# Scatters of routed rows issued one by one, each behind a read of Y, instead of in bursts of four

## The chip, the cores and the metric

The kernel runs on one core of a Trainium2 chip. The metric is device time in microseconds: the median of three timed runs of the kernel before is 1020.86 us (1019.78 to 1023.98). TensorE multiplies matrices (its weight loads are shown apart, as PEld), VectorE (DVE) and ScalarE (ACT) work on tiles, GpSimd (POOL) does small fills and copies and issues indirect transfers, and SyncE (SP) issues the plain ones.

## The reference

Three stages in a row, in float32, on 4 x 768 = 3072 tokens:

- a recurrent attention: per head a 40 x 40 state is read by `r` (that gives the output `y`), then decayed by `w`, corrected by `a` and `b`, and gets `v k^T` added, token by token;
- a mixture of experts: each row of 320 goes through the one of 8 experts (320 to 1024 to 320, ReLU) that has the largest of 8 logits, and is scaled by its probability and an output gate;
- a shared block, 320 to 2048 to 320, with a learned slope for negative values.

```
y[:, :, t] = einsum('bhd,bhde->bhe', rt, state)
logits = x @ w_gate;  e_idx = argmax(logits, axis=1)
out[mask] = gate_w[mask, None] * eom[mask, e, None] * (maximum(x[mask] @ w1[e], 0) @ w2[e])
```

## The kernel before

**Attention.** The recurrence is cut into 12 chunks of 64 tokens; each chunk is done in two halves of 8 (batch, head) pairs a side. That makes 24 steps, and `slot(s)` (line 717) is called for s = 0 to 24: it does the state part of step s and the read part (Y) of step s - 1, which I call the Y part of step s. For the first sixteen steps it also prepares step s + 8 (cumulative decays, triangular factors, and the inversion of 32x32 blocks, `tmp` and `S`, lines 668 and 669, which VectorE does in small pieces between the rest). The inversion's tile S is cleared by GpSimd (lines 658 and 659) once in four steps. From step 17 on (`LATE`) there is nothing more to prepare.

In the Y part TensorE transposes (`XT`, line 757), multiplies by R (`MY`, line 766) and forms two masked products (`pp`, lines 770 and 771, VectorE writes them into the tile x); after the state part's products `R` (lines 687, 728 and 789) and `W` (line 739, from `rh`, which ScalarE evicts, line 731) it adds the rest of MY (line 809). VectorE then updates the state (`tm` and `mc`, lines 714 and 715) and reads Y out of PSUM into `yt` in two halves (line 814). The next loads of X and R (lines 692 and 702) are issued by SP at that place. Next comes the R product of the next step (line 728), which waits for `yt` and for the state.

**Routing inside the scan.** Every second chunk completes 256 rows a half; `unit` (line 116) turns them into rows of 320 and their logits: TensorE multiplies (line 123), VectorE sums the logits (line 124), ScalarE copies the rows into a buffer `xu` (line 126, a ring of four). `route` (line 128) returns the work on four such units as a list of small jobs: find the best expert, count with a triangular matrix, `place` (each row's position in its expert's list), four scatters, `sums` and `scale`. A scatter (line 174) is one indirect transfer by GpSimd of 128 rows of 320 floats to the DRAM array `xs`, followed by a memset of one element, `gap`. The jobs wait in the queue `rq`, and `slot` takes a few at its end (lines 842 to 845): a step takes `best`, the next `count`, the next `place` and then up to three scatters, the next the fourth scatter and `sums`, the next `scale`. From step 17 one more job is taken in the middle of a step (line 783). So the scatters of a group of four units are issued in one burst; there are five such groups. The last two groups, of two units each, are routed in step 24 and after it.

**After the scan.** `xload(0)` (line 198) is called after step 23 and loads the rows of expert 0 from `xs`; it waits for all scatters issued so far. GpSimd copies their last columns (line 207), TensorE transposes them (line 374), and the experts follow. Weights are loaded by SP (line 297) into three raw buffers from step 20 on and split into two parts by ScalarE, VectorE or GpSimd (lines 300 and 301).

The order of the instructions on each engine is the order in which the program issues them; waits between engines follow from the tiles that they read and write.

Of the kernel before, what the change touches and what calls it, by code (L numbers as in the profile page):

```python
# [11 lines left out]
F32 = mybir.dt.float32  # L12
# [16 lines left out]
NST = 2 * NCH  # L29
NUN = 2 * NCH  # L30
# [42 lines left out]
class Moe:  # L73
# [6 lines left out]
    def init(s,ap,rp):  # L80

        nc=s.nc; cp=s.cp; a=s.a; s.rp=rp

        s.wg=ap.tile([128,4,96],F32,name="wg")
        s.lg=rp.tile([128,8,16],F32,name="lg")
        s.pos=cp.tile([128,24],I32,name="pos"); s.sc=cp.tile([128,24],F32,name="sc")
        s.tot=cp.tile([128,NE+1],F32,name="tot"); nc.gpsimd.memset(s.tot,0.0)
        def iota(t,pattern,base=0,ch=0): nc.gpsimd.iota(t,pattern=pattern,base=base,channel_multiplier=ch,allow_small_or_imprecise_dtypes=True)
        s.nbk=-(-(NT-CB)//128)
        s.io=cp.tile([128,1],F32,name="io"); iota(s.io,[[0,1]],0,1)  # L90
        s.al=cp.tile([128,16],F32,name="al")
        s.scat=[]; s.gap=cp.tile([1,1],F32,name="gap"); s.xu={}
        s.oh=cp.tile([128,24,NE],F32,name="ohs"); s.pf=cp.tile([128,24],F32,name="pf")
        s.ids=cp.tile([128,24],I32,name="ids")
        nc.gpsimd.iota(s.ids,pattern=[[128,6],[768,4]],base=0,channel_multiplier=1)
        s.ido=rp.tile([128,24],F32,name="ido"); iota(s.ido,[[128,6],[768,4]],OVF,1)

        s.tri=rp.tile([128,128],F32,name="tri"); nc.gpsimd.memset(s.tri,1.0)
        nc.gpsimd.affine_select(out=s.tri,in_=s.tri,pattern=[[1,128]],base=-1,channel_multiplier=-1,compare_op=ALU.is_ge,fill=0.0)
        s.one=cp.tile([128,128],F32,name="one"); nc.gpsimd.memset(s.one,1.0)  # L100
        s.rev=rp.tile([128,NE],F32,name="rev"); iota(s.rev,[[-1,NE]],NE)
        s.base=rp.tile([128,NE],F32,name="base"); iota(s.base,[[CAP,NE]],CA+CB-CAP); nc.gpsimd.memset(s.base[:,0:1],0.0)
        s.end=rp.tile([128,NE],F32,name="end"); iota(s.end,[[CAP,NE]],CA+CB); nc.gpsimd.memset(s.end[:,0:1],float(CA))
# [12 lines left out]
    def unit(s,n,yt,ps,wk):  # L116
        nc=s.nc
        for u in range(2):

            t=ps.tile([128,512],F32,tag="ps",name="xtp"); tp=t[:,0:384].rearrange("t (p g) -> t p g",p=4)  # L120
            if n==22 and u==0:
                for _ in range(4): nc.tensor.matmul(t[:,384:512],s.ident,s.ident,start=True,stop=True)
            for p in range(4): nc.tensor.matmul(tp[:,p],yt[:,4*u+p],s.wg[:,p],start=True,stop=True)  # L123
            nc.vector.tensor_reduce(s.lg[:,(n+u)%8],tp.rearrange("t p g -> t g p")[:,80:96],AX.X,ADD)
            x=s.xu[n+u]=s.rp.tile([128,D],F32,name=f"xu{u}") if n+2==NUN else wk.tile([128,D],F32,tag="xu",name="xu",bufs=4)
            nc.scalar.copy(x.rearrange("t (p d) -> t p d",p=4),tp[:,:,0:80])

    def route(s,n0,n1,ps,wk):

        nc=s.nc; N=n1-n0; V=nc.vector; last=n1==NUN; sx=f"{n0}" if n0>=NUN-4 else ""  # L130
        if sx: wk=s.rp
        t={}
        def T(nm,k=NE):
            t[nm]=wk.tile([128,N,k] if k else [128,N],F32,tag="rt_"+nm+(sx if nm=="ex" else ""),name=nm,bufs=1)
            return t[nm]
        lg=s.lg[:,n0%8:n0%8+N]; l=lg[:,:,0:NE]; z=lg[:,:,NE:]
        bc=lambda x: x.unsqueeze(2).to_broadcast([128,N,NE])
        bm=lambda x: x.unsqueeze(1).to_broadcast([128,N,NE])
        f=lambda x: x.rearrange("p n e -> p (n e)")
        oh=s.oh[:,n0:n1]  # L140
        def best():
            if n0==4*(NCH//2-1):

                V.tensor_copy(s.tot[:,NE:NE+1],s.tot[:,0:1]); V.memset(s.tot[:,0:1],0.0)
                V.memset(s.base[:,0:1],float(CA)); V.memset(s.end[:,0:1],float(CA+CB))
            mx=T("mx",0); V.tensor_reduce(mx,l,AX.X,ALU.max)
            d=T("d"); V.tensor_tensor(d,l,bc(mx),SUB)
            v=T("v"); V.scalar_tensor_tensor(v,d,0.0,bm(s.rev),ALU.is_equal,MUL)
            m2=T("m2",0); V.tensor_reduce(m2,v,AX.X,ALU.max)
            V.tensor_tensor(oh,v,bc(m2),ALU.is_equal)  # L150
        def count():
            pr=s.mp.tile([128,2,N,NE],F32,tag="tp",name="pr") if last else ps.tile([128,2,N,NE],F32,tag="ps",name="pr")
            nc.tensor.matmul(f(pr[:,1]),s.one,f(oh),start=True,stop=True)
            nc.tensor.matmul(f(pr[:,0]),s.tri,f(oh),start=True,stop=True)
            c=t["pr"]=wk.tile([128,2,N,NE],F32,tag="rt_pr",name="prs",bufs=1)
            nc.scalar.copy(c,pr)
            nc.scalar.activation(T("ex"),t["d"],AF.Exp)
            v=T("v"); V.tensor_tensor(v,oh,bm(s.end),MUL)
            V.tensor_reduce(T("le",0),v,AX.X,ADD)
        def place():  # L160
            pr=t["pr"]

            run=wk.tile([128,N+1,NE],F32,tag="rt_run",name="run",bufs=1)
            V.tensor_tensor(run[:,0],s.tot[:,0:NE],s.base,ADD)
            for i in range(N):
                V.tensor_tensor(run[:,i+1],run[:,i],pr[:,1,i],ADD)
            rk=T("v"); V.tensor_tensor(rk,pr[:,0],run[:,0:N],ADD)
            V.tensor_tensor(rk,rk,oh,MUL)
            pf=s.pf[:,n0:n1]; V.tensor_reduce(pf,rk,AX.X,ADD)
            m2=T("m2",0); V.tensor_tensor(m2,pf,t["le"],ALU.is_ge)  # L170
            V.tensor_tensor(m2,m2,s.ido[:,n0:n1],MUL)
            V.tensor_tensor(s.pos[:,n0:n1],pf,m2,ALU.max)
            V.tensor_tensor(s.tot[:,0:NE],run[:,N],s.base,SUB)
        def scatter(n):
            i=nc.gpsimd.indirect_dma_start(out=s.xs,out_offset=IOA(s.pos[:,n:n+1]),in_=s.xu.pop(n),in_offset=None)

            for o in s.scat: s.tc.declare_no_dep(i.ins,o.ins,reason="distinct rows")
            s.scat.append(i)
            nc.gpsimd.memset(s.gap,0.0)
        def sums():  # L180
            zz=T("zz"); V.tensor_tensor(zz,z,oh,MUL)
            V.tensor_reduce(T("zs",0),zz,AX.X,ADD)
            sm=T("sm",0); V.tensor_reduce(sm,t["ex"],AX.X,ADD)
            V.tensor_scalar(sm,sm,1e-9,None,ADD)
        def scale():
            ez=T("ez",0); nc.scalar.activation(ez,t["zs"],AF.Exp,scale=-1.0)
            V.scalar_tensor_tensor(ez,ez,1.0,t["sm"],ADD,MUL)
            V.reciprocal(s.sc[:,n0:n1],ez)
        return [(0,best),(0,count),(0,place)]+[(1,lambda n=n: scatter(n)) for n in range(n0,n1)]+[(1,sums),(2,scale)]

    def rows(s,e):
        o,n=((0,CA),(CA,CB))[e//NE] if e%NE==0 else (CA+CB+CAP*(e-1),CAP)
# [345 lines left out]
def attention(ctx,octx,tc,a,m,ident,rp):  # L538
# [178 lines left out]
    def slot(s):  # L717
# [31 lines left out]
        if Y:  # L749
# [3 lines left out]
            for sd in range(2):  # L753
# [2 lines left out]
                for qq in range(4):  # L756
                    nc.tensor.transpose(XT[:,qq],x1[bl,sd,qq,64:192],ident[bl,bl])
                nc.scalar.copy(xt[:,:,192*sd:192*sd+64],XT)
            if not B: route(1000); units()

            MY=[ps.tile([P,2,208],F32,tag="ps",name="MY") for _ in range(2)]
            def y2(t): return bass.AP(t.tensor,t.offset,[*t.ap[:-1],(144,2),(1,64)])
# [4 lines left out]
            def pp(sd):  # L767
                Pp=ps.tile([P,8,64],F32,tag="ps",name="Pp")
                for qq in range(4):
                    nc.tensor.matmul(Pp[:,2*qq:2*qq+2],xt[:,qq,128*sd:128*sd+128],rz1[:,:,qq,sd],start=True,stop=True)  # L770
                nc.vector.tensor_tensor(p4(x1[:,sd]),Pp.rearrange("p (a j) t -> p a j t",j=2),mask.unsqueeze(1).unsqueeze(1).to_broadcast([P,4,2,64]),MUL)  # L771
            def p4(t): return bass.AP(t.tensor,t.offset,[t.ap[0],(232,4),(PO[1]-PO[0],2),(1,64)])
            ym(0,YA)
            if not B: route(1)
# [29 lines left out]
        if Y:  # L804
# [8 lines left out]
            for b in range(2):  # L813
                i=nc.vector.tensor_tensor(v4(yt[:,4*b:4*b+4,cs]),y2(MY[b]),v4(e1[:,4*b:4*b+4,0:64]),MUL)
                if n2 is None: fence[0]=i
            if not B:
                while rq and rq[0][1].__name__!='sums': route(1)
            if s+1<NST: loadX(s+1); loadR(s+1)
# [24 lines left out]
        route(1)  # L843
        for _ in range(3):
            if rq and rq[0][0]==1: route(1)
    ready=[]; rq=deque(); YA=4
    def units():
        while ready:
            c2,up,yt=ready.pop(0)
            m.unit(4*c2+2*up,yt,ps,wk)  # L850
            n=4*c2+2*up+2
            if up or c2==5:
                new=m.route(n-(4 if c2<5 else 2),n,ps,wk)

                k=len(new)-2 if n==NUN else 0
                for j in reversed(new[:k]): rq.appendleft(j)
                rq.extend(new[k:])
    def route(n):
        for _ in range(min(n,len(rq))): rq.popleft()[1]()
# [82 lines left out]
```

## Time and profile before

| what | value |
|---|---|
| median of three timed runs | 1020.86 us |
| profiled execution, its own time | 1029.33 us |
| its span, first to last instruction | 1027.6 us |
| mean granted TensorE clock | 0.946 |
| TensorE, VectorE, ScalarE, GpSimd busy | 958.8, 779.2, 398.3, 148.5 us |
| scan with routing | about the first 430 us |

The profile page gives busy time by engine and the costliest groups of instructions; the trace behind it answers questions on a stretch of time. In a timeline row the first number is the start in microseconds from the span's start, the second the time that the row covers, then the engine, the line, the operation, output and inputs by name, the shapes and the count; in brackets stand the idle time of the engine before it and what ended it. [...] A row of a step begins with the window (from the start of one step's first `yt` product to the start of the next step's) and its length; the steps shown are 8, 9, 12, 16, 17, 19, 20, 21 and 23, and counts stand in brackets behind the busy times. "issue" is time in which an engine waited for nothing that the profile shows.

### The profile page before, as it was taken

The numbers are of one execution on the slowest core, as the hardware profiler recorded it, in microseconds if no ns is written. First come the engines' busy times: TensorE is split into PE (matmuls) and PEld (weight loads), VectorE is DVE, ScalarE is ACT, GpSimd is POOL, SyncE is SP. The second block draws the span as 40 slices with busy tenths as digits, with TensorE's granted clock in tenths as the row PEclk, the third lists the DMA queues.
The fourth block names the chain that finished last, engine by engine and source line by source line (L and its number), as shares of the span: only waits on it lengthen the run. The fifth ranks groups of instructions, "written<-read, shape, count | busy, mean of one in ns | idle before, by whom it ended". The sixth has DMA issues, their size and how long they took to land.

```text
span 1027.6 us, 26866 instructions
## 1 busy us (share of the span) xinstructions
PE 958.8 (93%) x11172; PEld 873.2 (85%) x11172; DVE 779.2 (76%) x1898; ACT 398.3 (39%) x816; POOL 148.5 (14%) x224
## 2 busy tenths in 40 slices
PE   5469999898998999999999999899999999999998
PEld 5458888787887888889999999778999999999997
DVE  7999999999985734578888888577666667666664
ACT  3734545444551224355556555323222122212211
POOL 1000000201001100323444444310001010100000
PEclk8568999999996969999999999999999999999999
DMA  4334767434432334367777766540100000000000
GB/s 127 117 105 132 242 210 211 128 100 138 113 78 65 98 116 112 99 210 239 229 235 235 243 219 227 185 125 11 47 1 27 27 26 26 20 33 1 26 1 26
DMA packets 59391, 118.46 MB, mean 115 GB/s; under 512 B 7492, under 2 KB 34308, under 8 KB 59268
## 3 DMA queue, kind: packets, MB, share of 16 engines
q1 hardware_dynamic: 55220, 103.04, 33.0%
q0 software_dynamic: 4048, 13.69, 3.9%
q8 instruction: 88, 1.44, 0.6%
q14 instruction: 35, 0.29, 0.1%
HBM read 90.24 MB, written 26.46 MB: 114 GB/s over the span
## 4 chain that ended last, share of the span: by engine, by line
PE 71%; DVE 15%; DMA 5%; ACT 4%; issue 3%; SPq 1%; another core or an unknown queue 0%; POOL 0%; ACTq 0%; DVEq 0%; POOLq 0%
PE hp L385 25%; PE yp L412 24%; PE MY L809 3%; PE Pp L770 3%; PE xtp L123 2%; DVE S L669 2%; DVE tmp L668 2%; PE W L739 2%; PE R L687 2%; DMA rz<-R 2%; PE tp L374 2%; PE R L728 1%; DVE kf L609 1%; PE MY L766 1%; DVE x L771 1%
## 5 line engine op out<-in xcount | busy, mean ns | idle before, releaser
L385 PE MATMUL hp<-xh,w 128*128 128x512 f32 (+3 forms) x1008 | 298.4, 379 | 0.1
L412 PE MATMUL yp<-w,hh 128*128 128x320 f32 (+1 forms) x1280 | 284.4, 309 | 0.6 <-ACT hh L401 0.6
L412 PEld LDWEIGHTS yp<-w,hh 128*128 128x128 f32 (+1 forms) x1280 | 217.0, 186 | 12.6 <-ACT hh L401 2.3
L385 PEld LDWEIGHTS hp<-xh,w 128*128 128x128 f32 x1008 | 187.5, 189 | 25.7 <-issue 0.4
L412 PE MATMUL yp<-w,hl 128*128 128x320 f32 x584 | 181.4, 311 | 4.3 <-DVE hl L393 3.7
L401 ACT CAST hh<-g 128x512 fp32r<-128x512 f32 x96 | 59.6, 621 | 275.3 <-PE yp L412 148.3
L385 PE MATMUL hp<-xl,w 128*128 128x512 f32 (+3 forms) x336 | 126.1, 375 | 0.2 <-DVE xl L377 0.2
L402 DVE TENSOR_TENSOR hl<-g,hh 128x512 fp32r<-128x512 f32 x96 | 66.5, 692 | 72.9 <-ACT hh L401 72.1
L412 PEld LDWEIGHTS yp<-w,hl 128*128 128x128 f32 x584 | 109.7, 188 | 6.7 <-DVE hl L393 4.7
L399 DVE TENSOR_SCALAR g<-hp,al 128x512 f32<-128x512 f32 x96 | 71.9, 749 | 39.7 <-PE hp L385 39.6
L301 DVE TENSOR_TENSOR w<-raw,w 128x1024 fp32r<-128x1024 f32 (+3 forms) x65 | 88.3, 1360 | 16.7 <-ACT w L300 14.8
L669 DVE TENSOR_TENSOR S<-S,tmp 128x110 f32<-128x110 f32 (+19 forms) x336 | 69.6, 246 | 0.8
L668 DVE TENSOR_TENSOR tmp<-S 128x110 f32<-128x110 f32 (+19 forms) x336 | 69.3, 245 | 0.5
L400 DVE SCALAR_TENSOR_TENSOR g<-hp,g 128x512 f32<-128x512 f32 x96 | 66.4, 692 | 3.3
L385 PEld LDWEIGHTS hp<-xl,w 128*128 128x128 f32 x336 | 63.5, 189 | 5.4 <-DVE xl L377 0.6
L300 ACT CAST w<-raw 128x1024 fp32r<-128x1024 f32 (+1 forms) x66 | 64.2, 975 | 6.5 <-DMA raw<-W 6.4
L770 PE MATMUL Pp<-rz,xt 128*128 128x128 f32 x384 | 59.2, 300 | 0.0
L771 DVE TENSOR_TENSOR x<-Pp,mask 128x512 f32<-128x512 f32 x48 | 32.6, 685 | 34.7 <-PE Pp L770 26.8
L809 PE MATMUL MY<-x,kb 128*64 128x104 f32 (+1 forms) x768 | 47.1, 266 | 12.5 <-DVE x L771 9.0
L499 POOL DMA_INDIRECT xg<-xs,pos x24 | 25.5, 1062 | 226.9 <-PE tp L374 167.9
L742 ACT COPY x<-W 32x320 f32<-32x320 f32 x96 | 40.0, 417 | 38.8 <-PE W L739 36.3
L809 PEld LDWEIGHTS MY<-x,kb 128*64 128x64 f32 x768 | 39.5, 148 | 16.8 <-DVE x L771 11.6
(169 smaller groups left out, 1404.1 us busy)
## 6 DMA issues: line engine op xcount, KB each, us to landing
raw<-W SPq DMA_DIRECT2D x45, 512.0 KB
x<-VX SPq DMA_DIRECT2D x48, 232.0 KB
fm<-FM SPq DMA_DIRECT2D x46, 160.0 KB
xs<-z SPq DMA_DIRECT2D x5, 1440.0 KB
raw<-WI SPq DMA_DIRECT2D x10, 512.0 KB
raw<-WO SPq DMA_DIRECT2D x10, 512.0 KB
vv<-VM SPq DMA_DIRECT2D x24, 160.0 KB
rz<-R SPq DMA_DIRECT2D x48, 80.0 KB
```

The costliest lines, as they stand in the source:

```text
L300: s.nc.scalar.copy(hi,r[0][:,0:n])
L301: (eng or s.nc.vector).tensor_tensor(lo,r[0][:,0:n],hi.bitcast(F32),SUB)
L385: for i,(l,r) in enumerate(seq): nc.tensor.matmul(hp,l,r,start=(i==0),stop=(i==len(seq)-1))
L399: nc.vector.tensor_scalar(g,hp,0.0,s.al[:,f:f+1],ALU.min,MUL)
L400: nc.vector.scalar_tensor_tensor(g,hp,0.0,g,ALU.max,ADD)
L401: nc.scalar.copy(hh,g)
L402: nc.vector.tensor_tensor(hl,g,hh.bitcast(F32),SUB)
L412: nc.tensor.matmul(yp[j][o],l,r[:,f],start=(f==0 and i==0),stop=(f==nf-1 and i==len(p)-1))
L668: V.tensor_tensor(t3[:,r],S[:,r,j:j+1].to_broadcast([P,n,w]),S[:,j:j+1,j+1:].to_broadcast([P,n,w]),MUL)
L669: for r in rows: V.tensor_tensor(S[:,r,j+1:],S[:,r,j+1:],t3[:,r],ADD)
L770: nc.tensor.matmul(Pp[:,2*qq:2*qq+2],xt[:,qq,128*sd:128*sd+128],rz1[:,:,qq,sd],start=True,stop=True)
L809: nc.tensor.matmul(MY[q//4][64*sd:64*sd+64,q//2%2,104*(q%2)+o:104*(q%2)+o+w1],kb1[:,q,64*sd:64*sd+64],x1[:,sd,q//2,128*(q%2)+o:128*(q%2)+o ...
```

## The change

Groups that end at unit 20 or before (the five groups of four) no longer return their scatters as jobs. `place` puts them into a queue of their own, `s.sq`. `spread` takes one of them: GpSimd first copies one element of a tile into `gap`, which makes it wait for the instruction that writes that element, and then issues the scatter. It is called after the first of the two `yt` products of each step, with an element of `yt`; in steps 22 and up also after the first masked product, with an element of x. At the end of steps 22 and 23 one more scatter is issued without such a copy. With the queue filled at the end of steps 7, 11, 15, 18 and 22 that makes one scatter in each of steps 8 to 21 and three each in steps 22 and 23. `sums` follows `place` in the job list. The ring of row buffers `xu` has eight tiles instead of four.

```diff
-        s.scat=[]; s.gap=cp.tile([1,1],F32,name="gap"); s.xu={}
+        s.scat=[]; s.sq=deque(); s.gap=cp.tile([1,1],F32,name="gap"); s.xu={}
...
-            x=...wk.tile([128,D],F32,tag="xu",name="xu",bufs=4)
+            x=...wk.tile([128,D],F32,tag="xu",name="xu",bufs=8)
...
-        return [(0,best),(0,count),(0,place)]+[(1,lambda n=n: scatter(n)) for n in range(n0,n1)]+[(1,sums),(2,scale)]
+        sc=[lambda n=n: scatter(n) for n in range(n0,n1)]
+        if n1<=20: return [(0,best),(0,count),(0,lambda: (place(),s.sq.extend(sc))),(1,sums),(2,scale)]
+        return [(0,best),(0,count),(0,place)]+[(1,f) for f in sc]+[(1,sums),(2,scale)]
+    def spread(s,at):
+        if s.sq:
+            s.nc.gpsimd.tensor_copy(s.gap,at); s.sq.popleft()()
...
 in pp(sd), after the masked product:
+                if s>=NST-2 and sd==0: m.spread(x1[0:1,0,0,0:1])
...
             for b in range(2):
                 i=nc.vector.tensor_tensor(v4(yt[:,4*b:4*b+4,cs]),y2(MY[b]),v4(e1[:,4*b:4*b+4,0:64]),MUL)
                 if n2 is None: fence[0]=i
+                if b==0: m.spread(yt[0:1,0,64*(c1%2):64*(c1%2)+1])
...
         for _ in range(3):
             if rq and rq[0][0]==1: route(1)
+        if s>=NST-2 and m.sq: m.sq.popleft()()
```

## Rows read from the trace of the kernel before

**Rows 1.** The page, busy time, share of the span and instructions of TensorE.

```profile
PE 958.8 (93%) x11172; PEld 873.2 (85%) x11172; DVE 779.2 (76%) x1898; ACT 398.3 (39%) x816; POOL 148.5 (14%) x224
```

**Rows 2.** Nine steps: length; busy PE, PEld, DVE, ACT, POOL; clock, DMA share, GB/s.

```profile
177.50:194.88 17.38, 14.90 (x325) 13.14 (x323) 15.20 (x53) 6.97 (x17) 5.22 (x14) 1.00 0.44 134
194.88:211.78 16.90, 14.63 (x292) 12.92 (x291) 16.76 (x65) 7.39 (x19) 0.00 (x0) 0.90 0.39 105
...
238.31:255.40 17.09, 14.09 (x323) 12.58 (x321) 15.23 (x53) 6.97 (x17) 4.98 (x14) 1.00 0.45 132
...
298.92:317.76 18.84, 15.52 (x314) 13.23 (x313) 11.03 (x46) 6.97 (x17) 5.00 (x14) 0.87 0.29 86
317.76:337.66 19.90, 19.90 (x263) 18.20 (x263) 12.43 (x61) 4.83 (x12) 0.00 (x0) 0.61 0.20 51
...
350.30:365.49 15.19, 12.08 (x254) 10.97 (x252) 8.37 (x33) 3.56 (x9) 4.31 (x8) 0.83 0.37 109
365.49:384.44 18.95, 18.40 (x264) 16.56 (x261) 4.08 (x13) 3.98 (x10) 0.00 (x0) 0.59 0.44 137
384.44:396.86 12.42, 12.42 (x258) 11.35 (x258) 4.78 (x12) 5.37 (x12) 0.00 (x0) 1.00 0.43 124
...
408.93:420.74 11.81, 10.12 (x216) 8.34 (x212) 5.16 (x18) 3.58 (x10) 4.54 (x8) 1.00 0.47 137
```

**Rows 3.** Timeline of GpSimd: scatters of the third, fourth and last burst.

```profile
308.37 0.97 POOL L175 DMA_INDIRECT xs<-xu,pos  x1 [1.91 <-ACT mt L799]
...
312.17 1.00 POOL L175 DMA_INDIRECT xs<-xu,pos  x1 [0.21 <-issue]
...
358.78 0.96 POOL L175 DMA_INDIRECT xs<-xu,pos  x1 [0.22 <-issue]
...
412.69 1.30 POOL L175 DMA_INDIRECT xs<-xu,pos  x1 [52.86 <-ACT xt L758]
...
416.83 0.96 POOL L175 DMA_INDIRECT xs<-xu,pos  x1 [0.22 <-issue]
```

**Rows 4.** Chain of waits in the third burst: start us, us, what.

```profile
309.51 0.42 issue
309.94 0.28 PE MY L809
...
310.67 0.25 PE MY L809
...
314.27 2.68 PE MY L809 x26
```

**Rows 5.** Timeline of the fourth burst.

```profile
355.78 0.76 PE L789 MATMUL R<-x,n 32*32 32x40 f32 x32
...
360.76 0.44 ACT L731 ACTIVATE rh<-R 128x320 f32<-128x320 f32 x1 [5.10 <-remote]
...
361.25 1.27 PE L739 MATMUL W<-rh,tt 32*32 32x40 f32 x32 [2.96 <-ACT rh L731]
```

**Rows 6.** Timeline of the fifth burst.

```profile
415.06 0.76 PE L789 MATMUL R<-x,n 32*32 32x40 f32 x30 [0.19 <-ACT x L742]
...
418.82 0.44 ACT L731 ACTIVATE rh<-R 128x320 f32<-128x320 f32 x1 [3.81 <-PE MTp L797]
```

**Rows 7.** Timeline behind the Y read of step 18.

```profile
352.33 0.44 ACT L731 ACTIVATE rh<-R 128x320 f32<-128x320 f32 x1 [3.53 <-PE R L728]
...
354.00 0.76 PE L739 MATMUL W<-rh,tt 32*32 32x40 f32 x32
```

**Rows 8.** Timeline from step 23 to expert 0: load, copy and transposes of its rows.

```profile
420.86 0.58 SPq L203 DMA_DIRECT2D xa<-xs  x1
...
425.72 0.34 POOL L207 COPY xa<-xa 128x192 f32<-128x192 f32 x1 [7.84 <-DMA xa<-xs]
...
431.13 1.15 PE L374 MATMUL tp<-ident,xa 128*128 128x128 f32 x9
```

**Rows 9.** All scatters: ns min, median and max, first and last start.

```profile
L175 POOL DMA_INDIRECT xs<-xu,pos x24: 959/964/1298, 188.1 to 440.3; - x24
```

More of the change, by code (lines that the diff above doesn't have):

```diff
@@ L124, in unit @@
             nc.vector.tensor_reduce(s.lg[:,(n+u)%8],tp.rearrange("t p g -> t g p")[:,80:96],AX.X,ADD)
-            x=s.xu[n+u]=s.rp.tile([128,D],F32,name=f"xu{u}") if n+2==NUN else wk.tile([128,D],F32,tag="xu",name="xu",bufs=4)
+            x=s.xu[n+u]=s.rp.tile([128,D],F32,name=f"xu{u}") if n+2==NUN else wk.tile([128,D],F32,tag="xu",name="xu",bufs=8)
             nc.scalar.copy(x.rearrange("t (p d) -> t p d",p=4),tp[:,:,0:80])
@@ L758, in slot @@
                 nc.scalar.copy(xt[:,:,192*sd:192*sd+64],XT)
-            if not B: route(1000); units()
+            if not B:
+                route(1000); units()
             MY=[ps.tile([P,2,208],F32,tag="ps",name="MY") for _ in range(2)]
```

## The prediction, made before the kernel was run

> **What bounds the kernel now.** The page first: TensorE is busy for 93% of the span [rows 1], so a saving must shorten a stage in which TensorE waits or runs slowly. The change touches only the attention scan with its routing, the first 430 us, so I read that stretch by steps: one window per step s, ending at the start of the step's first read of Y (line 814, the product `yt`) [rows 2]. Up to step 15 VectorE fills the step (16.76 of 16.90 us in step 9); from step 16 TensorE does (12.42 of 12.42 in step 21). Three things stand out. Steps 8 and 12 leave VectorE idle for 2.18 and 1.86 us, step 9 for 0.14. Steps 17 and 20 take 19.90 and 18.95 us, at a granted clock of 0.61 and 0.59, where step 21 with much the same work takes 12.42 at 1.00. Steps 16, 19 and 23 are longer than TensorE's busy time in them by 3.32, 3.11 and 1.69 us.
>
> All of these lie on or right behind one of five bursts of four scatters, which GpSimd issues in steps 8, 12, 16, 19 and 23; its timeline shows them [rows 3] (the third from 308.37, the last from 412.69; steps 8 and 12 have theirs at 188.1 and 248.8). One scatter is some 0.96 us and the next starts 1.27 us after it ((312.17 - 308.37) / 3), so a burst takes 5 us. The chain of waits shows what TensorE does meanwhile: in the third burst it is through with `R` at 309.51, then gives out one or two matmuls every 0.7 us, with "issue" before each, until 314.27, which is 1.1 us after the last scatter's end [rows 4]. In the fourth, the second R product ends at 356.54, but ScalarE, which waits for it, starts only at 360.76, 1.0 us after the burst's end, and TensorE idles 2.96 us for that [rows 5]. In the fifth ScalarE starts at 418.82 after a product that ended at 415.82 [rows 6]. So whatever TensorE issues or signals comes through late from some time in a burst until 1 us after its end. [...]
>
> **Part by part: what goes.** Without the bursts:
> - Steps 8 and 12: VectorE's idle time falls from 2.18 and 1.86 to step 9's 0.14: 2.0 + 1.7.
> - Step 16: TensorE would begin MY at 309.5 and need some 1.7 us; VectorE has inversion work queued till about 312.7, then `tm` and `mc`, some 1.2 us: `yt` starts at 313.9 and not 317.76: 3.9. Step 17 then runs at the higher level; its VectorE load is 12.43 and a full step of TensorE is 12.42, so 13.0 for 19.90: 6.9.
> - Step 19: 15.19 becomes its TensorE time of 12.08 and a little, 12.3: 2.9. Step 20 becomes step 21, 12.42 for 18.95: 6.5.
> - Step 23: 11.81 becomes 10.12: 1.7.
>
> Sum 25.6 us. VectorE is next late in steps 8, 12, 16 and 17, TensorE in the others.
>
> **What comes.** The same twenty scatters: one per step behind `yt` of steps 8 to 21, three each in steps 22 and 23. A burst's first scatter is the nearest row for a single one. If the hold runs to 1 us after its end, it lasts 2.0 us from its start. In the third burst TensorE ran freely for 1.14 us of that (until 309.51), so 0.9 us would be lost; in the fifth it ran freely for 3.1 us (until 415.82), so nothing. A gain is excluded, since a scatter takes no work from TensorE.
> - Steps 8 to 15, eight scatters: behind `yt` VectorE has long work of its own and TensorE waits for it; nothing. If that cover were gone, 8 x 0.9 = 7.
> - Steps 16 to 23, twelve scatters: between 0 and 0.9 each. Behind `yt` of step 18 ScalarE has `rh` done at 352.77, and TensorE's W comes to it at 354.00 [rows 7], so that signal may be 1.2 us late for nothing. I take a third of the bound, 0.3 each: 3.6. If all of each hold were on the path, 2.0 each: 24.
> - Expert 0's rows are loaded after the last of the twenty. Now the last scatter ends at 417.79 [rows 3], the load is issued at 420.86, GpSimd's copy of its rows starts at 425.72 and TensorE's transposes of them at 431.13 [rows 8]. After the change the last two scatters start behind `yt` of step 23 (420.74) and end at about 423.5; with the same distances the load is issued at 426.6, the copy starts at 431.5 and ends at 431.8, the transposes start at 432: 0.9 late. Bounds 0 (hidden in what step 24 loses anyway) and 2 (if the raw weights, queued on SP behind this load, slip with it). I take 1.0.
> - The copy of one element ahead of each scatter stands in no row: between nothing and the 0.34 of the 128x192 copy [rows 8], on an engine that idles 52.86 us before the last burst [rows 3]. It waits for `yt`; queued behind it on GpSimd are the inversion's memsets of S, which need a transpose that VectorE comes to later, and in step 24 the copy of expert 0's rows, counted above. Nothing. In steps 22 and 23 the load of X into the tile that the copy reads must wait for GpSimd, us before SP comes to it: nothing, at most a scatter's 0.96 twice.
> - The four small VectorE instructions of `sums` go one step earlier, unchanged in number: nothing. Eight row buffers for four: ScalarE's copies into them meet scatters some four steps old: nothing, as now.
> - SP's queue keeps its order; X and R are issued right at `yt`, so each single transfer (128 rows of 1280 bytes) meets them. They are used in the middle of the next step or later: nothing; if they land late, up to 0.5 each in steps 16 to 23, 4 in all.
>
> Sum: 25.6 - 3.6 - 1.0 = 21.0 us off a profiled execution of 1029.33 (span 1027.6, 1.7 around it).
>
> **From the profiled execution to the timed one.** It is 8.5 us above the median, 1020.86. That excess may lie anywhere, or in the bursts (a lower clock that not each run meets). I put half of it there: 21.0 - 4.2 = 16.8, so 1004. With none of it there 1000, with all 1008.
>
> **Rivals.**
> 1. The bursts' price is the profile's own, or only moves to other steps: the time stays, 1021, from 1016 to 1026. For it: the hold is seen on the engine with most instructions [rows 1]. Against it: then timed runs would be 25 us below the profiled one; they are 8.5 below, which bounds that share. [...]
> 2. Slower: the clock. The two bursts that cost most did so by what came after: a step at the lower level costs 6.5 (step 20 against 21). A single scatter now stands behind `yt` in every step from 16 on, where TensorE's next product waits for that `yt`. If each takes the full 2 us from TensorE, the level may stay low in steps 17 to 21: 5 x 6.5 = 32.5, plus 1.0 at the tail, less 25.6: +7.9, 1029. It decides from the fourth such step on (26 against 25.6). Against it: in steps 8, 12 and 23 the engines lost some 2 us and the clock stayed at 1.00 [rows 2].
> 3. Singles become long. The median scatter is 964 ns and the longest 1298 [rows 9], with VectorE busy beside most of them; 0.33 more for each of twelve is 4 us: 1008. [...]
> 4. It does not spread: six of the twenty still come in steps 22 and 23, two pairs of them back to back. If these hold as the fifth burst does, its 1.7 stay: 1005.5.
>
> **How the numbers follow.** Forecast with its sizes (993 to 1012, rivals 3 and 4 in it) 0.60; a smaller gain, 1012 to 1016, 0.05; rival 1, 0.20; rival 2 and other losses over 0.5%, 0.15. A measurement of this kernel tells 0.5%, about 5 us, from no change: faster 0.65, same 0.20, slower 0.15. The low end is all of 25.6 with free singles, 995, less 2 for a shorter step 17: 993. The high end takes in the no-change case and twelve holds of 2.0 us (24 + 1 against 25.6, 1021), up to 1025.
>
> **What would show it.** Right: by steps cut at `yt`, no granted clock under 0.8 in steps 16 to 22, step 17 near 13 us, 19 and 20 near 12.4; no "issue" before MY in step 16; on GpSimd scatters one by one, each under 1.3 us. Singles dearer than thought: ScalarE or VectorE starting over 0.7 us after the product that it waits for in the 2 us behind a scatter, and "issue" before R or MY there. Tail: TensorE's first transposes of expert 0 waiting for GpSimd's copy. The prediction is wrong if the profiled execution loses its slow steps and the timed median doesn't move (rival 1), or if low steps stay without bursts (rival 2).

## The result

| | before | after |
|---|---|---|
| median, us (runs, lowest to highest) | 1020.32 (4, 1015.87 to 1023.98) | 1005.06 (4, 1002.06 to 1008.41) |
| profiled execution, us | 1029.33 | 1002.83 |
| span of it, us | 1027.6 | 1001.1 |
| mean granted clock of it | 0.946 | 0.971 |

The median before is of four runs, the three known ahead of the prediction and one of 1015.87. The ratio of the times is 0.985, with a 95% interval of 0.9812 to 0.9888: 15.3 us faster, where 16.8 were forecast (1004). The profiled executions lie 26.5 us apart. The first row of the page after answers to [rows 1]; TensorE's busy time, which counts a slow clock (step 17: 19.90 us at 0.61 before, 13.84 at 0.88 after), has fallen by 20.4 us.

```profile
PE 938.4 (94%) x11172; PEld 855.0 (85%) x11172; DVE 778.5 (78%) x1898; ACT 397.8 (40%) x816; POOL 155.0 (15%) x242
```

The same steps as in [rows 2] (8, 12, 16, 17, 19, 20, 23), with the same columns, in the changed kernel:

```profile
177.08:193.27 16.19, 13.79 (x322) 12.28 (x320) 15.61 (x56) 6.96 (x17) 0.75 (x6) 1.00 0.46 129
...
236.04:252.30 16.26, 14.10 (x322) 12.45 (x321) 15.68 (x56) 6.96 (x17) 2.46 (x9) 1.00 0.48 136
...
295.05:311.37 16.32, 14.62 (x326) 12.99 (x324) 11.42 (x50) 6.96 (x17) 1.97 (x9) 1.00 0.35 95
311.37:326.02 14.65, 13.84 (x256) 12.50 (x256) 11.62 (x57) 4.52 (x12) 1.28 (x3) 0.88 0.21 53
...
337.79:348.29 10.50, 10.35 (x256) 9.38 (x253) 9.19 (x39) 3.87 (x10) 1.25 (x3) 1.00 0.41 111
348.29:360.63 12.34, 11.79 (x263) 10.67 (x259) 3.29 (x9) 3.66 (x9) 1.23 (x3) 1.00 0.70 221
...
385.30:394.76 9.46, 8.91 (x213) 7.97 (x210) 5.95 (x24) 3.78 (x11) 4.45 (x8) 1.00 0.54 152
```

Column 1 less that of [rows 2] gives where the time went: 1.2 us in step 8, 0.8 in 12, 2.5 in 16, 5.3 in 17, 4.7 in 19, 6.6 in 20, 2.4 in 23. Over steps 8 to 15 it is 3.45 and over 16 to 24 it is 22.1; everything else in the span makes 0.9. The column before the last two is the granted clock, TensorE's share of its full speed: steps 16 and 20 are back at 1.00, step 17 is not (0.88). The prediction's lower level is 0.50 here: the profile of before has it from 315 to 333 us, in steps 16 and 17, and 1.00 from 333.5 to 340.

GpSimd's timeline in step 19 shows the new pattern: the copy that waits for Y, 0.56 us later the scatter, and nothing behind it. The second line is the longest scatter of all (1.91 us, in step 23).

```profile
338.34 0.18 POOL L194 COPY gap<-yt 1x1 f32<-1x1 f32 x1 [9.98 <-DVE yt L821]
339.07 0.98 POOL L175 DMA_INDIRECT xs<-xu,pos  x1 [0.56 <-issue]
...
388.99 1.91 POOL L175 DMA_INDIRECT xs<-xu,pos  x1 [1.34 <-ACT xt L763]
```

And this is what that scatter of step 19 does to TensorE and ScalarE:

```profile
338.59 1.13 PE L733 MATMUL R<-mc,g 64*64 64x40 f32 x32 [0.15 <-DVE yt L821]
...
341.06 0.44 ACT L736 ACTIVATE rh<-R 128x320 f32<-128x320 f32 x1 [4.77 <-PE XT L762]
...
341.58 0.76 PE L744 MATMUL W<-rh,tt 32*32 32x40 f32 x32
```

R is through at 339.72; ScalarE's `rh`, which reads R alone, starts 1.34 us later, 1.0 us after the scatter's end at 340.05. (The row names XT as what it waited for, but that product is behind R and was through at 340.12.) With the scatters left out (e4 below) the `rh` of step 17 starts 0.11 us after its R (313.17 to 313.28). So a lone scatter can delay a signal too, as the prediction took it from [rows 5, 6]. But W comes from TensorE's queue only at 341.58, behind work that it has anyway: step 19 takes 10.50 us, and 10.41 without scatters, so the delay costs 0.1 us.

### The profile page after: what moved, and what is told of

The parts are those of the page before. It is cut to its first block, busy times and chain, and to the rows that moved or that the text cites. A ratio compares the mean times of both kernels' runs of the same rounds, so it can differ in the third digit from the quotient of the medians.

```text
span 1001.1 us, 26895 instructions
## 1 busy us (share of the span) xinstructions
PE 938.4 (94%) x11172; PEld 855.0 (85%) x11172; DVE 778.5 (78%) x1898; ACT 397.8 (40%) x816; POOL 155.0 (15%) x242
## 4 chain that ended last, share of the span: by engine, by line
PE 66%; DVE 22%; DMA 5%; issue 4%; ACT 2%; POOL 0%; SPq 0%; DVEq 0%; ACTq 0%; POOLq 0%
PE hp L390 24%; PE yp L417 24%; DVE S L674 4%; DVE tmp L673 4%; PE MY L816 3%; PE Pp L776 3%; DVE F L604 2%; DVE kf L614 2%; PE tp L379 2%; PE W L744 2%; DVE x L777 1%; PE MY L772 1%; DVE w L306 1%; PE R L733 1%; PE xtp L123 1%
## 5 line engine op out<-in xcount | busy, mean ns | idle before, releaser
L776 PE MATMUL Pp<-rz,xt 128*128 128x128 f32 x384 | 55.3, 287 | 0.0
L816 PE MATMUL MY<-x,kb 128*64 128x104 f32 (+1 forms) x768 | 43.7, 255 | 10.4 <-DVE x L777 10.4
L395 ACT ACTIVATE hh<-hp 128x448 fp32r<-128x448 f32 (+2 forms) x72 | 36.6, 508 | 37.2 <-issue 25.0
L816 PEld LDWEIGHTS MY<-x,kb 128*64 128x64 f32 x768 | 36.7, 140 | 14.1 <-DVE x L777 13.0
```

The lines of the kernel that those rows point to most:

```text
L816: nc.tensor.matmul(MY[q//4][64*sd:64*sd+64,q//2%2,104*(q%2)+o:104*(q%2)+o+w1],kb1[:,q,64*sd:64*sd+64],x1[:,sd,q//2,128*(q%2)+o:128*(q%2)+o ...
```

## Experiments

The prediction's theory (1): a burst of four scatters holds TensorE, until 1 us after the last one. Against it stood that the gain comes from what else the change does (A: the ring of eight rows, the earlier `sums`), and later a narrower one (2): not the burst, but that one scatter starts right behind another. Step lengths from each profile, in us, with the granted clock of step 17; "pause" is the time from a scatter's end to the next one's start in the bursts of steps 16 and 19 (those of steps 8 and 12 are given with e9 and e10).

| kernel | pause | 16 | 17 (clock) | 19 | 20 | 23 | 8 to 15 | 16 to 24 | median |
|---|---|---|---|---|---|---|---|---|---|
| before | 0.31 | 18.84 | 19.90 (0.61) | 15.19 | 18.95 | 11.81 | 121.42 | 129.10 | 1020 to 1023 |
| after | alone | 16.32 | 14.65 (0.88) | 10.50 | 12.34 | 9.46 | 117.97 | 106.99 | 1005.06 |
| e1, no tie | 0.86 | 15.38 | 13.16 (1.00) | 11.52 | 12.18 | 11.41 | 120.04 | 110.48 | 1009.94 |
| e2, first groups spread | 0.31 | 19.80 | 14.31 (0.98) | 14.28 | 18.76 | 11.83 | 118.42 | 122.26 | 1022.77 |
| e3, last groups spread | alone | 15.23 | 16.80 (0.70) | 10.41 | 12.34 | 9.45 | 120.09 | 109.03 | 1006.38 |
| e4, none | | 15.28 | 14.64 (0.88) | 10.41 | 12.34 | 9.52 | 118.19 | 105.74 | 1000.84 |
| e5, five constants | 1.30 | 14.62 | 13.42 (1.00) | 10.72 | 12.18 | 10.38 | 118.54 | 104.98 | 1002.28 |
| e6, no tie, no copy | 0.31 | 18.50 | 19.96 (0.60) | 15.13 | 14.58 | 12.19 | 119.85 | 125.83 | 1022.66 |
| e7, matmuls in the stall | alone | 16.31 | 13.56 (1.00) | 10.41 | 12.34 | 9.45 | 118.03 | 105.80 | 1005.14 |
| e8, after again | alone | 16.31 | 16.88 (0.70) | 10.41 | 12.35 | 9.46 | 118.02 | 110.10 | 1006.18 |
| e9, two constants | 0.86 | 14.64 | 13.41 (1.00) | 12.78 | 18.41 | 11.02 | 120.97 | 113.26 | 1009.78 |
| e10, one wide constant | 0.81 | 15.29 | 13.42 (1.00) | 11.58 | 12.17 | 11.06 | 118.21 | 107.17 | 1005.23 |
| e11, plain transfers | 0.03 to 0.06 | 14.65 | 13.42 (1.00) | 10.41 | 12.34 | 9.52 | 118.17 | 103.61 | 1002.59 |
| e12, mix | 1.30 | 14.64 | 13.43 (1.00) | 10.86 | 12.18 | 9.53 | 118.24 | 103.90 | 1001.52 |

**e1: the tie taken away.**

```diff
     def spread(s,at):
         if s.sq:
-            s.nc.gpsimd.tensor_copy(s.gap,at); s.sq.popleft()()
+            s.nc.gpsimd.memset(s.gap,0.0); s.sq.popleft()()
```

> The changed kernel with one edit: the small GpSimd operation ahead of each spread scatter writes a constant and no longer reads Y, so that nothing holds a scatter back to a step; the ring of eight rows, the earlier sums and the places of the scatters in GpSimd's program order stay. Theory 1 (four scatters in a row hold TensorE's issue and its signals until about 1 us after the last one; the spreading is the whole gain): the scatters run four in a row again as soon as the positions stand, steps 16 to 23 get back most of their 22 us, median 1015 to 1022. Rival A (the ring of eight rows and the earlier sums made the gain): about 1005, step lengths as after the change though the scatters stand in bursts.

It took 1009.94 us (1009.41 to 1010.09; ratio to before 0.9899, 0.9838 to 0.9961): neither. The scatters do run four in a row again, yet steps 16 to 20 stay short. GpSimd and TensorE in the third burst:

```profile
306.98 0.97 POOL L175 DMA_INDIRECT xs<-xu,pos  x1 [1.90 <-ACT mt L806]
...
308.02 1.82 PE L816 MATMUL MY<-x,kb 128*64 128x104 f32 x27
...
308.81 0.96 POOL L175 DMA_INDIRECT xs<-xu,pos  x1 [0.62 <-ACT x L747]
...
310.15 0.45 PE L816 MATMUL MY<-x,kb 128*64 128x104 f32 x5 [0.31 <-issue]
...
310.62 0.96 POOL L175 DMA_INDIRECT xs<-xu,pos  x1 [0.63 <-issue]
```

Where [rows 4] show one or two matmuls of MY every 0.7 to 1.4 us, 27 run in one go here, with 0.31 us lost. The difference to see is the pause: the constant that replaces the copy brings 0.86 us between two scatters, where [rows 3] have 1.27 from start to start, 0.31 of it pause. Of these later bursts only in that of step 23, where the last scatter came 0.30 us behind the third, did the matmuls of MY come in small groups again (15, 3, 5 and 9 of them); step 24 ran at a clock of 0.68 and took 10.59 us for 7.28. That gave theory 2.

**e2 and e3: only some groups spread.** One line each, `if n1<=8: return [...]` (groups 0 and 1) and `if 8<n1<=20: return [...]` (groups 2 to 4), for `if n1<=20: return [...]`; the other groups go in bursts.

> The changed kernel with only the first two groups of rows (0 to 7) spread; the other three groups go in bursts of four as before. Theory 1 with the step lengths measured: only the 3.4 us of steps 8 to 15 stay gained, steps 16 to 23 are as before: median 1015 to 1018, 10 to 13 us above the changed kernel. Rival A (the ring of eight, not the spreading): about 1005. Rival B (the profile's own price: an execution without a trace pays nothing for a burst, the timed gain comes from elsewhere): within 2 us of the changed kernel.

> The changed kernel with the first two groups of rows (0 to 7) in bursts of four as before, the other three spread. Theory 1: the first two bursts cost what steps 8 to 15 lost before the change, 3.4 us: median 1006 to 1010, steps 16 to 23 as after the change. Rival C (in the first steps VectorE bounds and a burst there is hidden; the shorter steps 8 to 15 come from the sums that moved): within 1 us of the changed kernel, 1003 to 1006.

e2 took 1022.77 us in ten runs (1014.37 to 1027.52), ratio 1.0003 (0.9968 to 1.0037), more than the 1015 to 1018 expected. It has the ring of eight for all groups, so the ring alone gives nothing. Its steps 8 to 15 are 3.0 us shorter than before, which its time doesn't show within that interval. Its step 17 shows that a burst's loss isn't always followed by the low clock: after 19.80 us of step 16, step 17 took 14.31 at 0.98, where [rows 2] have 19.90 at 0.61. e3 took 1006.38 (1003.65 to 1008.27; 0.9857, 0.9793 to 0.992), 1.3 above the changed kernel, which doesn't tell theory 1 from rival C; by its profile the two early bursts cost 2.1 us. The timed gain lies in the last three groups.

**e4: no spread scatters.** The queue isn't filled: `(0,place)` for `(0,lambda: (place(),s.sq.extend(sc)))`.

> The changed kernel with its twenty spread scatters left out (the first 20 blocks of routed rows never reach the buffer in DRAM, so that the result's rows are wrong); their positions are still computed. It gives what the spread scatters still cost. Theory 1 (a single scatter's hold ends before TensorE's next matmul is ready, all but hidden): 0 to 3 us below the changed kernel, 1002 to 1005. Rival D (every scatter holds TensorE for about its own 1 us wherever it stands): 12 to 20 us below, 985 to 993.

1000.84 us (999.80 to 1002.61; 0.9808, 0.9747 to 0.9869). The median lies 4.2 us under the changed kernel's, more than the 0 to 3 expected, though the intervals of the two ratios overlap. Step by step its profile is the changed kernel's within 0.3 us, but for step 16 (1.04 us less). There the scatter behind Y of step 15 (296.28 to 297.24) stretches L from 1.16 to 1.50 us and makes ScalarE wait. First the changed kernel:

```profile
295.56 1.50 PE L628 MATMUL L<-g,kf 64*64 64x64 f32 x64
...
296.28 0.96 POOL L175 DMA_INDIRECT xs<-xu,pos  x1 [0.50 <-ACT kb L646]
...
297.59 1.03 PE L733 MATMUL R<-mc,gx 64*64 64x40 f32 x28 [0.40 <-issue]
...
297.83 0.37 ACT L633 ACTIVATE nt<-L 32x256 f32<-32x256 f32 x1 [1.52 <-PE L L628]
```

and the same place without scatters:

```profile
295.93 1.16 PE L628 MATMUL L<-g,kf 64*64 64x64 f32 x64
...
297.15 0.37 ACT L633 ACTIVATE nt<-L 32x256 f32<-32x256 f32 x1 [0.48 <-PE L L628]
```

**e5: the bursts kept, the pause made longer.** The kernel before with one edit:

```diff
             s.scat.append(i)
-            nc.gpsimd.memset(s.gap,0.0)
+            for _ in range(5 if n<20 else 1): nc.gpsimd.memset(s.gap,0.0)
```

> The kernel before with one edit: behind each of the first twenty scatters GpSimd writes its one-element constant five times, not once, so that the scatters of a burst stand some 0.8 us apart and not 0.3; the bursts of four, the ring of four rows and the order of the sums stay as before. In the first experiment the bursts that had come to stand 0.85 us apart held TensorE hardly at all. Theory 1, as predicted (a burst of four holds TensorE until 1 us after its last scatter): the bursts last 2.2 us longer, so the kernel is slower than before by up to 8 us, 1020 to 1030. Theory 2 (the hold comes from a scatter that starts right behind the one before, and a gap of 0.85 us does without): steps 16, 17, 19, 20 and 23 are as short as in the changed kernel, median 1002 to 1009. Rival A (sums and ring): as before, about 1021.

1002.28 us (1001.80 to 1004.16; 0.9851, 0.9827 to 0.9876): with bursts of four, the old ring and the old order, the whole gain. In its fourth burst, the second and the third scatter, and TensorE beside the third:

```profile
342.84 0.96 POOL L175 DMA_INDIRECT xs<-xu,pos  x1 [0.62 <-ACT rh L731]
343.81 0.67 POOL L179 MEMSET gap<- 1x1 f32 x5
345.10 0.96 POOL L175 DMA_INDIRECT xs<-xu,pos  x1 [0.62 <-ACT x L742]
```
```profile
344.53 1.13 PE L687 MATMUL R<-vv,ka 64*64 64x40 f32 x32
345.59 1.29 PE L809 MATMUL MY<-x,kb 128*64 128x64 f32 x32
```

No "issue" stands there. Theory 1, which had this kernel slower than before, is wrong as put; so is A.

**e6: the first experiment with the short pause.** e1 less its constant: `s.sq.popleft()()` alone.

> The first experiment's kernel (the changed kernel without the tie to Y) less the small GpSimd operation ahead of each scatter, so that one constant written stands between two scatters, as in the kernel before; ring of eight and earlier sums stay. Theory 2 (the gap decides): where the scatters stand 0.2 to 0.3 us apart TensorE is held again, steps 16 to 23 lose 15 to 22 us, median 1015 to 1023. Theory 3 (the order of the sums or of the program, not the gap, made the first experiment fast): about 1010, as it was there.

1022.66 us in nine runs (1016.84 to 1031.71; 1.0019, 0.998 to 1.0059), and 1033.33 in a tenth. One GpSimd instruction fewer per scatter, 0.31 us of pause in place of 0.86, and steps 16 to 24 lose 15.4 us against e1:

```profile
299.14:317.64 18.50, 15.73 (x314) 13.25 (x313) 11.63 (x50) 6.98 (x17) 5.01 (x14) 0.88 0.30 87
317.64:337.60 19.96, 19.96 (x262) 18.18 (x262) 11.96 (x57) 4.74 (x12) 0.00 (x0) 0.60 0.19 50
```

So theory 2 holds both ways for bursts of four, and ring and `sums` without a pause give nothing.

**e7 and e8: the stall ahead of step 17.** e8 is the changed kernel unchanged; e7 adds `if s==16: heat(10)` behind `units()`, ten matmuls that nobody reads.

> The changed kernel with ten 128x128 matmuls of the identity, whose result nobody reads, put into step 16 where TensorE idles for VectorE (1.8 us, after which the granted clock fell to 0.5 to 0.77 for some 5 us). Theory: the clock stays up in step 17 (13.2 us as in the first experiment, not 14.65): 1.5 us under the changed kernel in its profile, 1000 to 1004 as median. Rival: the matmuls delay the step's first read of the state or the stall moves: 1004 to 1009.

> The changed kernel once more, on the same chip and in the same rounds as the other three of this call: 1002 to 1008.5, its two groups of times being one step at the low clock apart.

In the changed kernel TensorE waits 1.79 us for VectorE's `yt` of step 16, and the clock falls (the windows' columns are those of the steps):

```profile
312.18 1.22 PE L733 MATMUL R<-mc,gx 64*64 64x40 f32 x32 [1.79 <-DVE yt L821]
```
```profile
310.50:312.20 1.70, 0.02 (x2) 0.02 (x2) 1.67 (x7) 0.00 (x0) 0.18 (x1) 1.00 0.88 204
312.20:315.00 2.80, 2.80 (x50) 2.61 (x52) 2.80 (x18) 1.76 (x6) 1.10 (x2) 0.66 0.46 151
315.00:318.00 3.00, 3.00 (x50) 2.42 (x47) 0.46 (x4) 0.68 (x3) 0.00 (x0) 0.75 0.02 3
```

In e8 the same stall (1.80 us) cost more: 16.88 us at 0.70. With the matmuls in it step 17 took 13.56 at 1.00, as expected, but the whole took 1005.14 us (1004.17 to 1006.13) beside 1006.18 (1004.07 to 1011.49) for e8. The profile of e7 lost behind the scan what it won in step 17 (clock 0.93 between 600 and 700 us, where the changed kernel's had 0.98). The time is the rival's (1004 to 1009): as a gain e7 is not shown. The stall goes with the earlier `sums`: kernels with `sums` in their old place (e5, e9 to e12) have 13.4 us in step 17 at 1.00, while e4, with no scatter but the earlier `sums`, has the stall (1.78 us) and 14.64. Steps 16 and 17 together take 29.92 us in e4 and 28.07 in e11 and e12 (e12 has the ring of eight too), so the earlier `sums` costs 1.9 us there. (e1, with the earlier `sums` too, waited 1.12 us there and kept the clock.) In e5, `sums` runs behind `yt` (from 314.75) and TensorE waits 0.81 us:

```profile
311.77 1.13 PE L728 MATMUL R<-mc,gx 64*64 64x40 f32 x32 [0.81 <-DVE yt L814]
```

**e9 and e10: how long, and what, the pause must be.** The kernel before with `range(2 if n<20 else 1)` in e5's edit, and with one constant of 128x640 elements in the place of the small one.

> The kernel before with the one-element constant written twice behind each of the first twenty scatters, not once (five times in the fifth experiment). If the second constant brings the longer pause with it that stood between scatters in the first and the fifth experiment (0.62 us ahead of a scatter in place of 0.21), the scatters stand some 0.85 us apart and TensorE is not held: steps 16, 17, 19, 20 as in the fifth experiment, median 1001 to 1006. If the pause needs more time or more instructions, they stand 0.35 us apart and TensorE is held as before, 1016 to 1025.

> The kernel before, and behind each of the first twenty scatters GpSimd writes one constant of 128x640 elements (some 0.65 us of work by the rate of the 128x520 one, 0.53 us) in place of one element: one instruction between two scatters, as before the change, but the time of five. Theory 2a (what counts is the time between two scatters): TensorE not held, steps 16 to 23 as in the fifth experiment, median 1001 to 1006. Theory 2b (what counts is how many instructions stand between): held as before, and the bursts are longer, 1018 to 1030.

e9: 1009.78 us (1007.58 to 1012.28; 0.9863, 0.9829 to 0.9897); e10: 1005.23 (1002.48 to 1006.52; 0.9822, 0.9787 to 0.9858). One instruction of 0.65 us does as well as several small ones (e10's time is the one expected of 2a), so it is the time that counts and not the number. But 0.8 us is not quite enough: in e9 the hold comes back beside the fourth scatter (347.75 to 348.71). TensorE, then ScalarE:

```profile
346.19 0.89 PE L687 MATMUL R<-vv,ka 64*64 64x40 f32 x17
347.75 0.31 PE L687 MATMUL R<-vv,ka 64*64 64x40 f32 x4 [0.67 <-issue]
348.51 0.31 PE L687 MATMUL R<-vv,ka 64*64 64x40 f32 x4 [0.45 <-issue]
349.25 0.43 PE L687 MATMUL R<-vv,ka 64*64 64x40 f32 x7 [0.43 <-issue]
```
```profile
349.32 0.86 ACT L742 COPY x<-W 32x320 f32<-32x320 f32 x2 [3.36 <-remote]
```

After it step 20 ran at 0.63 and took 18.41 us. Both of my answers for e9 (the whole gain, or none) missed: the cost falls with the pause in stages. Between them the pause alone doesn't order the runs (e10 with 0.81 lost less than e9 with 0.86). Step 19 takes 14.3 to 15.2 us at 0.31, 11.5 to 12.8 at 0.81 to 0.86, 10.7 to 10.9 at 1.30, and 10.4 to 10.5 with scatters alone or none. The bursts of steps 8 and 12 agree: with pauses of 0.39 to 0.41 us there (e1, e9) steps 8 to 15 take 120.0 and 121.0 us, with 0.81 to 0.85 (e5, e10, e12) 118.2 to 118.5, and 118.2 without scatters.

**e11: plain transfers.** In the kernel before, `nc.gpsimd.dma_start(out=s.xs[128*n:128*n+128], in_=s.xu.pop(n))` for `n<20`, issued when the positions are there.

> The kernel before, in which the first twenty scatters are plain transfers that GpSimd issues (128 rows of 1.28 KB to consecutive places of the same buffer, so that the rows do not land where the routing wants them and the result's rows are wrong), four in a row at the same points. Theory X (the indirect scatter is what holds TensorE): steps 16 to 23 as short as in the fifth experiment, 998 to 1005. Theory Y (any GpSimd-issued transfer that stands right behind another holds it): losses in steps 16, 17, 19, 20 and 23 as before, 1015 to 1025.

1002.59 us (998.05 to 1005.52; 0.9796, 0.9754 to 0.9838). Four transfers of the same rows by the same engine, closer than the scatters ever stood, hold nothing: TensorE beside the fourth burst runs as in e4 (step 19: 10.41 us).

```profile
341.52 0.54 POOL L176 DMA_DIRECT2D xs<-xu  x1 [32.29 <-issue]
...
342.10 0.54 POOL L176 DMA_DIRECT2D xs<-xu  x1
...
342.69 0.54 POOL L176 DMA_DIRECT2D xs<-xu  x1
```
```profile
342.67 0.76 PE L792 MATMUL R<-x,n 32*32 32x40 f32 x32
343.37 1.16 PE L773 MATMUL Pp<-rz,xt 128*128 128x128 f32 x8
344.36 0.60 PE L800 MATMUL MTp<-ident,mc 128*128 128x128 f32 x4
```

So it is neither the bytes nor GpSimd's issuing as such, but the indirect form. That form differs in more than one way (0.96 us of GpSimd in place of 0.54, rows that land apart and not in a row); which of them does it wasn't tried.

**e12: both ways together.** The changed kernel with `if n1==20: return [...]` (only the last group spread) and `range(5 if n<16 else 1)` in e5's edit.

> The changed kernel in which the first four groups of rows go in bursts again, with five constants between scatters as in the fifth experiment, and only the last group is spread and tied (in the fifth experiment its burst cost steps 23 and 24 about 1.3 us more than in the changed kernel). Theory: the fifth experiment's steps 16 to 22 and the changed kernel's steps 23 and 24: 1000 to 1003, 1 to 2 us under the fifth experiment and 3 to 5 under the changed kernel. Rival: the low clock after step 16's stall comes back: 1003 to 1007.

1001.52 us in five runs (999.75 to 1003.03), ratio 0.979 (0.9761 to 0.9819), as expected: it is faster than before by 2.1%. The changed kernel's two sets of four runs, each beside its own runs of the kernel before, have ratios of 0.985 (0.9812 to 0.9888) and 0.989 (0.9848 to 0.9932); e12's interval meets the lower edge of the first and lies below the second. Steps 16, 19 and 23 of it:

```profile
295.55:310.19 14.64, 14.35 (x326) 12.78 (x323) 10.85 (x46) 6.96 (x17) 4.21 (x19) 1.00 0.33 89
...
335.12:345.98 10.86, 10.68 (x262) 9.56 (x259) 8.40 (x33) 3.67 (x9) 4.33 (x18) 1.00 0.45 130
...
382.64:392.17 9.53, 8.98 (x216) 8.04 (x212) 5.95 (x24) 3.86 (x11) 3.25 (x5) 1.00 0.48 132
```

## Why the prediction was right, and where not

The time, the sign and the places were right: steps 8, 12, 16, 17, 19, 20 and 23 gave 23.4 us in the profile (25.6 forecast), and what TensorE lost there did come from the scatters (e6 against e1, e11).

1. **The cause was put too wide.** "whatever TensorE issues or signals comes through late from some time in a burst" took a burst of four as the cause. e5 keeps the bursts and has the whole gain; what counts is the pause between the indirect scatters of a burst. The change works because it sets them apart, in steps 8 to 21 by a step's 10 to 16 us; the tie to Y is one way to do that, and not a needed one. [Rows 4] hinted at it: TensorE ran freely through the first scatter, and the first "issue" (309.51) stands just ahead of the second. But a short pause alone is not the whole cause either. The changed kernel keeps one pair 0.31 us apart, in step 24, and TensorE runs on beside it; the step takes 7.28 us, and 7.29 in e4:

```profile
396.05 0.96 POOL L175 DMA_INDIRECT xs<-xu,pos  x1 [0.56 <-ACT xt L763]
...
397.31 0.96 POOL L175 DMA_INDIRECT xs<-xu,pos  x1 [0.23 <-issue]
397.46 1.09 PE L772 MATMUL MY<-rz,mt 128*64 128x128 f32 x16
```

   TensorE gives out fewer instructions there (102 matmuls in the step, 256 in step 19). Whether that or the missing third scatter spares it wasn't tried.
2. **Step 17: forecast 13.0, measured 14.65 (16.88 in e8).** The step of the sum that failed is "The four small VectorE instructions of `sums` go one step earlier, unchanged in number: nothing." They stand in step 16 (304.83 to 305.53), where VectorE is the late one, ahead of `tm` and `yt`; TensorE's stall is 1.8 us, where kernels with `sums` in the old place have 0.8 (e5), and the clock fell after it. It cost 1.9 us in steps 16 and 17 (e4 against e11). Step 16 itself gave 2.5 of the 3.9; 1.0 of the rest is the single scatter in it (point 4).
3. **Step 19: forecast 2.9, measured 4.7.** TensorE's busy time of 12.08 in [rows 2] was taken as its work; some of that was work at the low clock (0.83). It is 10.35 at 1.00.
4. **Singles: 3.6 forecast, 1.25 measured in the profiles** (steps 16 to 24, changed kernel against e4), 1.04 of it in step 16. The medians lie 4.2 us apart; where the rest of that lies no profile shows. The bound of 0.9 for one was about right there; elsewhere the slack of some 1.2 us behind Y (352.77 to 354.00 in [rows 7]) covers it.
5. **Signs.** No clock under 0.8 was to come; step 17 had 0.88, and 0.70 in e8, behind the stall of point 2 and not behind a scatter. Six singles are longer than 1.3 us (194.7, 225.5, 237.3, 270.1, 284.5, 389.0; 1.45 to 1.91), so that sign was wrong, as rival 3 had it; the profile shows no cost of them (steps 9, 11, 12, 14, 15 and 23 are no more than 0.1 us over e4's). All six began while VectorE was in one instruction of 1.23 us (the scan of line 604, for 389.0 the product of line 306) and ended 0.77 to 1.00 us behind it, while a scatter that began 0.11 us ahead of such a scan took 0.99. No edit tried whether the one makes the other longer.

```profile
283.92 1.23 DVE L604 TENSOR_TENSOR_SCAN F<-fm,ones 128x520 f32<-128x520 f32 x1
284.47 1.46 POOL L175 DMA_INDIRECT xs<-xu,pos  x1 [0.49 <-issue]
```

6. **The tail: 1.0 forecast, 0.2 measured.** The load of expert 0's rows is issued 1.7 us after the last scatter's end, not the 3.1 of before, and GpSimd's copy is done 1.1 us before TensorE comes to the transposes (405.33, or 3.29 us after Y of step 24, where it was 3.11):

```profile
400.00 0.58 SPq L208 DMA_DIRECT2D xa<-xs  x1
...
403.86 0.34 POOL L212 COPY xa<-xa 128x192 f32<-128x192 f32 x1 [5.50 <-DMA xa<-xs]
...
405.33 1.20 PE L379 MATMUL tp<-ident,xa 128*128 128x128 f32 x9
```

7. **From the profile to the median.** "I put half of it there" was the wrong size: of the profiles' 26.5 us the medians show 15.3. The 11.2 between are the 9.0 by which the profile of before lies above its median and the 2.2 by which that of after lies below. The part of the profile behind step 24 is 599.6 us before, 599.1 after and 598.7 to 602.5 in the experiments, so the 9.0 hardly lie there. All of the excess may belong to the bursts, by their low clock, which comes and goes: step 17 took 19.90 before and 14.31 in e2, step 20 took 18.95 and 14.58 (e6), each behind such a burst. That the forecast is only 1.5 us off the measured gain is luck in part: this term was 7.0 us too small and the net 5.5 too small (21.0 forecast, 26.5 measured), and the two nearly cancel.

Rival 1 is out: the timed medians moved with the profiles in e5, e6 and e11. Whether an execution without a trace has the same hold, or a smaller one, these runs can't say. Rival 2 (a clock that stays low in steps 17 to 21) did not come, rival 4 neither: step 23 is as short as in e4, and of its two pairs one came 1.4 us apart and the other, in step 24, cost nothing (point 1).

## What to carry to other kernels

When engines seem to be held by a burst of indirect transfers, put a pause between the transfers before moving them: five one-element writes per scatter gave here what the queue and the ties gave. A trace shows the victim (TensorE's "issue", ScalarE starting 1 us after the last scatter), and only an edit of the pause alone, both ways, shows the cause. An order change that costs no work can still put work ahead of the engine that is late in that step, and a stall of 1.8 us there cost up to 3.5 us more by the clock behind it (step 17: 16.88 us at 0.70 in e8, 13.42 at 1.00 in e11).

## What the hardware showed

- Bursts of four indirect scatters of 0.96 us held TensorE's issue when the next began 0.31 us behind, in part at 0.81 to 0.86, hardly at 1.30. One pair 0.31 us apart, beside few matmuls, held nothing. Plain transfers of the same rows from the same engine didn't hold it either, some 0.05 us apart. What in the indirect ones holds it is open.
- In the bursts of steps 16 to 23 GpSimd starts a scatter 0.21 us after one small constant, but 0.62 after two or five (e9, e5) and 0.16 after one of 0.65 us (e10); in those of steps 8 and 12 it takes 0.16 to 0.17 after two or five as well. That accident gave e1 its pause; its reason wasn't tried.
- Six lone scatters that began inside a VectorE instruction of 1.23 us took 1.45 to 1.91 us in place of 0.96.
- A stall of 1.8 us of TensorE was followed by 14.65 us of step 17 in one execution and 16.88 in another of the same program; one of 0.8 (e5) by none.
